# Order of work around eight points of a one-core kernel: attention and two gated products

## The chip, the core and the metric

The kernel runs on one core of a Trainium2 chip. The metric is device time in microseconds (us). A core has TensorE (PE in the profile; PEld is its weight load), VectorE (DVE), ScalarE (ACT), GpSimd (POOL) and SyncE (SP, which here only issues DMAs). Each engine works through its own list of instructions in order and waits on semaphores for the others. SBUF is the on-chip memory; a matmul writes into one of the eight banks of PSUM, from which ACT or DVE must copy the result out before the bank is used again.

## What is computed

All data is float32. Attention over chunks of 32 queries (4 batches, 8 heads, 768 positions, 64 wide), each chunk against 8 memory keys and a window of 56 keys, is followed by two gated layers over the 3072 tokens:

```python
scores = scale * np.matmul(q_c, k_full.transpose(0, 1, 3, 2))
a = np.exp(scores - max); a = a / (sum + 1e-9)
out[:, :, c_start:c_end] = np.matmul(a, v_full)
...
a = x @ w1;  b = x @ w2          # 512 -> 1024
x = (a * b @ w3) @ w_out         # 1024 -> 1024 -> 512
...
a = x @ w_a; b = x @ w_b         # 512 -> 1536
return a * b @ w_out2            # 1536 -> 512
```

## The kernel before, in words

**Precision.** A float32 operand is split into a high part (a copy rounded by ACT, `split_hi`, L103) and a low part (DVE or POOL subtracts the high part, `split_lo`, L106). A product is three passes of matmuls: high by high, high by low, low by high (`PASSES`, pairs of weight part and data part).

**Weights** arrive as raw 64-bit words. A block is loaded by SP (`w_load`, L374 for the 1 MB blocks of the first stage, L368 to L371 for the 512 KB blocks of `w1` and `w2`), scaled by two ACT instructions (`w_scale`, L389 and L390), joined by two DVE instructions (`w_bits`, L394 and L395), and, where parts are needed, split (L431 on ACT, L425 on DVE). `w_tick` moves each block one step; calls to it stand at fixed places in the program. `BUFS["raw2"]` gives the buffers for raw 1 MB blocks.

**Stage 1** multiplies `w3` by `w_out` once: two halves of eight steps `k`, four banks each (`wps`). The first half consumes eight 1 MB blocks of `w3a`, which the text calls r0 to r7, the second four blocks of `w3b`, r8 to r11, each for two steps. Half-steps are counted by `g`. After a half, ACT and DVE copy its four banks out (`w_evict`, L559 and L560).

**Attention** is cut into 16 units `u` of two groups and run in slots that are strewn between the products of the stages (`attn_slot`). In order, a unit loads keys (`kraw`, L122), queries (`q`, L129, one buffer) and values (`v`, L142 and L148), copies the keys (DVE, L158), makes scores (PE, `sc`), takes the maximum, subtracts, exponentiates and norms (L196, L199, L210, L218 to L221), transposes (PE, `pt`, L232), copies that out of its banks (ACT, `p`, L238), multiplies with the values (PE, `xp`) and splits the result into the layer's data `xt` (ACT L103, DVE L106).

**Stage 2** (tiles 0 to 3 of 512 tokens): eight `ab_step`s per tile, each two products `psA` and `psB` of twelve matmuls (`ab_half`), their gate, and then the second product `psY`. `between` is called after each half and runs a weight tick and attention slots.

**Stage 3** (tiles 4 and 5 as a pair) uses seven half-size products for the pair in place of eight (`seven12`, `product`, L892). It goes through the hidden dimension in two halves `h`. Each half ends with eight groups j of `psY`; the second half adds what the first one stored. Meanwhile `x_build` loads the next stage's data and splits it (L714 load, L722 subtraction, L103, L106).

**Stage 4** (three pairs of tiles): twelve blocks `f` per pair, each seven products p0 to p6 of six matmuls (`seven`) into banks `pa`, `pb`, `pc`, the gate (`times`, L1081 DVE, L1082 ACT, L1083 POOL), and `out_part` (`ops`). In a block, `copied` (ACT, L904) brings p0 out of its bank for p2 to start in it, and again p2 and p3; `plus` (DVE, L1076) does the other banks. `w7_hi` and `w7_lo` split the weights of the next block, and `other` advances a generator of side work.

The program is written out by hand in this order; no scheduler changes it. SP's list is in order too: a load that waits for its buffer holds all loads behind it.

Of the kernel before, what the change touches and what calls it, by code (L numbers as in the profile page):

```python
# [7 lines left out]
F32 = mybir.dt.float32  # L8
# [5 lines left out]
P = 128  # L14
# [9 lines left out]
TT = 512  # L24
# [14 lines left out]
CH = 512  # L39
BUFS = {"raw64": (3, 0), "raw2": (0, 4), "dec": (4, 3)}  # L40
SPLIT = 2
# [5 lines left out]
def tile_attention_moe(  # L47
# [32 lines left out]
    def dram_tile(n, shape):  # L80
        return dram.tile(shape, F32, name=n, tag=n)

    yd = [dram_tile(f"yd{i}", [P, KD, TT]) for i in range(NT1)]
    xd = {i: dram_tile(f"xd{i}", [P, KD, TT]) for i in range(ND, NT1)}

# [207 lines left out]
    for u in range(NA):  # L293
        t0, t1, t2, t3 = SLOTS.get(u, (8, 8, 11, 12))
        for s, stage_of in (
            (t0, a_trans),
            (t1, a_pt),
            (t3, a_x),
            (t2, a_pv),
            (t2, lambda u: a_v(u + 1)),  # L300
            (0, a_scores),
            (0, lambda u: a_q(u + 1)),
            (int(u > 0), a_max),
            (2, a_norm(0)),
            (2 + (u > 0), a_norm(1)),
            (int(u > 0), a_exp(0)),
            (int(u > 0), a_exp(1)),
        ):
            at(BASE[u] + s, (stage_of, u))
        if u > 0:  # L310
            at(BASE[u] - 3, (a_keys, u))
            at(BASE[u] - 2, (a_k, u + 1))
    at(0, (a_v, 0))
    NEED = []
# [4 lines left out]

    def attn_slot(n=1):  # L320
        for _ in range(n):
            s = acount[0]
            if s >= NEED[-1]:
                return
            acount[0] += 1
            for stage_of, u in todo.get(s, []):
                stage_of(u)

# [233 lines left out]
    for half in range(2):  # L562
        banks = [psd.tile([P, 512], F32, tag="d", name="wps") for _ in range(4)]
        for k in range(8):
            for m in range(4):
# [12 lines left out]
                if half == 0:  # L578
                    if g >= 9:
                        attn_slot()  # L580
                    if g in (0, 2, 4, 6, 8, 9):
                        w_tick()
                    if g == 0:
                        a_k(0)
                        a_q(0)
                    if g == 7:
                        a_keys(0)
                        a_k(1)
                    if g == 9:
                        bound[0] = len(wsrc)  # L590
                    if g == 13:
                        w_turn()
                else:
                    attn_slot()
                    if g == 0:
                        w_next()
                    if g in (1, 4, 5, 6, 9, 10, 11, 12):
                        w_tick()
# [12 lines left out]
    def ab_half(ps, w, j, rhs):  # L611
        i = 0
        for k in range(KD):
            for a, b in PASSES:
                mm(ps[:, :TT], w[:, a, j, (k + 2 * j) % KD, :], rhs[:, b, k, :], i == 0, i == 3 * KD - 1)
                i += 1

# [65 lines left out]
    def between():  # L683
        nstep[0] += 1
        b = nstep[0] - NB * ti
        n = nstep[0]
        converting = any(pipe) or wraw
        if converting:
            w_tick()
        attn_slot(min(NEED[-1], NEED[0] + -(-(NEED[-1] - NEED[0]) * n // NA1)) - acount[0])  # L690
        if not converting:
# [196 lines left out]
    def product(ps, i, w, first):  # L888
        n = 0
        for k in range(2):  # L890
            for a, b in PASSES:
                nc.tensor.matmul(  # L892
# [82 lines left out]
    for t in range(ND, NT1, 2):  # L975
        for h in range(2):
# [11 lines left out]
            groups = [(n, i) for n in range(KD) for i in range(2)]  # L988
            ps_of, olds = {}, {}

# [13 lines left out]

            def y_old(j):
                if h == 1 and j < len(groups):
                    olds[j] = y_load(tmp(), yd, t + groups[j][1], groups[j][0])

            y_old(0)
            y_old(1)  # L1010
            y_old(2)
            for j, (n, i) in enumerate(groups):
# [10 lines left out]
                ps = ps_of.pop(j)[:, :TT]  # L1023
                if h == 0:
                    z = copied(ps)
                else:
                    z = olds.pop(j)
                    onto(z, ps, z, ALU.add)
                nc.sync.dma_start(out=yd[t + i][:, n, :], in_=z)
                y_old(j + 3)  # L1030
                if h == 1:
# [47 lines left out]
    def times(x, y, g2):  # L1079
        z = tmp()  # L1080
        nc.vector.tensor_tensor(z, x, y, ALU.mult)  # L1081
        nc.scalar.activation(g2[:, 0, :], z, AF.Copy)  # L1082
        nc.gpsimd.tensor_tensor(g2[:, 1, :], z, g2[:, 0, :].bitcast(F32), ALU.subtract)  # L1083

    def seven(w, g1, g2, other, after, lead):

        pa, pb = bank(), bank()
        product(pa, 0, w, True)
        s1 = copied(pa)
        product(pb, 1, w, True)  # L1090
        c11 = plus(pb, s1)
# [13 lines left out]
        c12 = plus(pc, u2)  # L1105
        w7_lo()
        other(1)
        product(pa, 6, w, False)
        after()
        times(pa, c11, g1)  # L1110
        times(c12, c22, g2)

    def out_part(ops, f, g2):
# [26 lines left out]
    next(cw)  # L1140

    def other(n):
        for _ in range(n):
            next(cw, None)

    seq = list(range(0, NT1, 2))
    for si, t in enumerate(seq):
# [16 lines left out]
        while len(fo) < M2:  # L1164
            next(cw)
        ops2 = out_new(psd, "d")
        out_part(ops2, 0, g2[0])
# [9 lines left out]
        if si == 0:  # L1177
            stagestack.close()


# [81 lines left out]
```

## Time and profile before

| | before |
|---|---|
| runs | 1062.44 us median of 3 (1061.69 to 1063.23) |
| profiled execution | 1062.38 us, of which the span from first to last instruction 1060.6 |
| PE busy | 1045.2 us of the span, granted clock 1.000 throughout |
| DVE, ACT, POOL busy | 591.4, 449.1, 245.6 us |
| DMA | 153 MB; 364 GB/s in the first fortieth of the span, 144 on average |

A row of the timeline gives start and length of a run of equal instructions on one engine, in us from the span's start; in brackets stands how long the engine was idle before and what ended it. "x48" counts instructions. A float32 matmul of stage 1 and of attention leaves two records.

### The profile page before, as it was taken

The page shows a single profiled execution, that of the slowest core. Times are in us where ns is not written, and L with a number is a line of the kernel's source. Part 1 is how long each engine was busy: PE and PEld are TensorE (multiplying, and loading weights), DVE is VectorE, ACT ScalarE, POOL GpSimd, SP SyncE. Part 2 cuts the span into 40 slices and gives each one's busy share as a digit, 9 for nine tenths or more (in the row PEclk, how much of TensorE's full clock was granted, in tenths as well). Part 3 has the DMA queues.
Part 4 walks back from the last instruction along what each step waited for, and adds up shares of the span by engine and source line. Part 5 has one row for each costly group of instructions (what it writes and reads, how often), then busy time and mean ns, then how long its engine had stood idle before and what let it go on. Part 6 is the DMA issues. An engine that isn't in the chain of part 4 may idle for free.

```text
span 1060.6 us, 18308 instructions
## 1 busy us (share of the span) xinstructions
PE 1045.2 (99%) x7394; PEld 835.6 (79%) x7394; DVE 591.4 (56%) x950; ACT 449.1 (42%) x789; POOL 245.6 (23%) x264
## 2 busy tenths in 40 slices
PE   9999999999999999999899999999999999999998
PEld 3447788888888888888688888888888888888886
DVE  5868956676675346357755565544444454444410
ACT  6655622444443334344455545333333334343310
POOL 0102398222322000000032233013332202222210
PEclk9999999999999999999999999999999999999999
DMA  9974467768885423235733333322222223222211
GB/s 364 316 195 154 150 206 228 248 227 277 273 292 179 138 85 113 74 118 177 218 123 110 109 117 115 120 75 76 98 71 70 94 97 109 69 70 70 70 40 40
DMA packets 74997, 153.15 MB, mean 144 GB/s; under 512 B 7968, under 2 KB 38048, under 8 KB 73632
## 3 DMA queue, kind: packets, MB, share of 16 engines
q1 hardware_dynamic: 66640, 118.90, 34.1%
q0 software_dynamic: 8064, 33.03, 9.6%
q8 instruction: 58, 0.95, 0.4%
q14 instruction: 27, 0.22, 0.1%
q10 hardware_dynamic: 208, 0.04, 0.0%
HBM read 116.83 MB, written 35.13 MB: 143 GB/s over the span
## 4 chain that ended last, share of the span: by engine, by line
PE 90%; DMA 3%; DVE 3%; issue 1%; ACT 1%; SPq 0%; DVEq 0%; ACTq 0%
PE ps L892 39%; PE ops L94 18%; PE psY L94 11%; PE psB L94 7%; PE psA L94 7%; PE wps L94 3%; PE xp L94 2%; PE sc L94 1%; DMA q<-in_qt 1%; DMA raw<-in_w 1%; DMA raw<-in_w3a 1%; PE pt L232 1%; DVE w L425 1%; DVE dec L395 0%; DVE x L106 0%
## 5 line engine op out<-in xcount | busy, mean ns | idle before, releaser
L892 PE MATMUL ps<-x,w 128*128 128x512 f32 x1848 | 425.8, 389 | 3.3 <-DVE tmp L908 2.0
L892 PEld LDWEIGHTS ps<-x,w 128*128 128x128 f32 x1848 | 346.5, 188 | 76.7 <-ACT tmp L904 2.2
L1076 DVE TENSOR_TENSOR tmp<-ps,tmp 128x512 f32<-128x512 f32 x108 | 74.6, 691 | 142.9 <-PE ps L892 131.6
L106 DVE TENSOR_TENSOR w<-w 128x512 fp32r<-128x512 f32 (+1 forms) x176 | 105.8, 619 | 82.8 <-ACT w L103 82.7
L904 ACT ACTIVATE tmp<-ps 128x512 f32<-128x512 f32 x132 | 78.7, 597 | 165.2 <-PE ps L892 155.2
L94 PE MATMUL psY<-g,wo 128*128 128x512 f32 x576 | 134.6, 391 | 0.0
L783 POOL DMA_DIRECT2D w<-wc x36 | 20.1, 559 | 466.9 <-PE ps L892 328.8
L94 PEld LDWEIGHTS psY<-g,wo 128*128 128x128 f32 x576 | 107.3, 188 | 22.6 <-DVE tmp L908 0.3
L94 PE MATMUL ops<-wo,g 128*128 128x512 f32 x504 | 118.6, 389 | 0.0
L94 PEld LDWEIGHTS ops<-wo,g 128*128 128x128 f32 x504 | 94.6, 188 | 19.6
L94 PE MATMUL psA<-xt,w 128*128 128x512 f32 x384 | 94.8, 395 | 0.8 <-DVE xt L106 0.5
L1083 POOL TENSOR_TENSOR g<-tmp,g 128x512 fp32r<-128x512 f32 x66 | 84.1, 1291 | 46.9 <-ACT g L1082 46.9
L94 PE MATMUL psB<-xt,w 128*128 128x512 f32 x384 | 93.9, 393 | 0.0
L103 ACT ACTIVATE w<-w 128x512 fp32r<-128x512 f32 (+1 forms) x176 | 92.1, 572 | 1.4 <-DMA w<-wd 1.4
L1082 ACT ACTIVATE g<-tmp 128x512 fp32r<-128x512 f32 x66 | 40.7, 633 | 109.9 <-DVE tmp L1081 109.9
L94 PEld LDWEIGHTS psA<-xt,w 128*128 128x128 f32 x384 | 70.8, 188 | 16.8 <-ACT xt L103 1.1
L94 PEld LDWEIGHTS psB<-xt,w 128*128 128x128 f32 x384 | 71.2, 188 | 15.0
L94 PE MATMUL ops<-fo,g 128*128 128x512 f32 x288 | 68.2, 389 | 0.0
L389 ACT ACTIVATE raw<-raw 128x512 f32<-128x512 f32 (+1 forms) x66 | 48.9, 741 | 33.3 <-DMA raw<-in_wab 17.2
L94 PEld LDWEIGHTS ops<-fo,g 128*128 128x128 f32 x288 | 54.1, 188 | 11.2
L94 PE MATMUL wps<-w_f 128*128 128x512 f32 x128 | 57.5, 599 | 0.2 <-DVE w_f L395 0.2
L103 ACT ACTIVATE x<-xb 128x512 fp32r<-128x512 f32 x56 | 32.2, 624 | 41.4 <-DVE xb L722 26.5
(74 smaller groups left out, 952.2 us busy)
## 6 DMA issues: line engine op xcount, KB each, us to landing
w<-wc POOLq DMA_DIRECT2D x36, 640.0 KB, 4.2
raw<-in_wab SPq DMA_DIRECT2D x24, 512.0 KB
v<-in_vw SPq DMA_DIRECT2D x64, 168.0 KB
w<-wc POOLq DMA_DIRECT2D x36, 256.0 KB, 3.8
kraw<-in_kt SPq DMA_DIRECT2D x16, 512.0 KB
raw<-in_w3a SPq DMA_DIRECT2D x6, 1024.0 KB
q<-in_qt SPq DMA_DIRECT2D x16, 384.0 KB
wc<-cs SPq DMA_DIRECT2D x12, 512.0 KB
```

What stands on the lines that cost most here:

```text
L94: nc.tensor.matmul(o, lhsT=l, rhs=r, start=first, stop=last)
L103: nc.scalar.activation(hi, src, AF.Copy)
L106: nc.vector.tensor_tensor(lo, src, hi.bitcast(F32), ALU.subtract)
L232: nc.tensor.transpose(pt[:, a // 4, a % 4, :], t[:, a].rearrange("p r k -> p (r k)"), id_sb)
L389: nc.scalar.activation(h, h, AF.Prelu, scale=2.0**-112, alpha=2.0**32)
L425: nc.vector.tensor_tensor(lo, a, hi.bitcast(F32), ALU.subtract)
L783: (nc.gpsimd if c else nc.sync).dma_start(out=t[:, 1, :C7].bitcast(F32), in_=wseq[n][:, :C7])
L892: nc.tensor.matmul(ps, lhsT=w[i][:, a, k, :], rhs=xs[i][:, b, k, :], start=first and n == 0, stop=n == 5, skip_group_check=not first,)
L904: nc.scalar.activation(z, ps, AF.Copy)
L1076: nc.vector.tensor_tensor(z, ps, y, ALU.add)
L1082: nc.scalar.activation(g2[:, 0, :], z, AF.Copy)
L1083: nc.gpsimd.tensor_tensor(g2[:, 1, :], z, g2[:, 0, :].bitcast(F32), ALU.subtract)
```

## The change

Eight edits in one file; line numbers after the first shift by one or more (L389 becomes L403 and so on).

1. `raw2`: three buffers for raw 1 MB blocks, not four.
2. In stage 1 three weight steps move: the one at `g == 13` of the first half to 14, those at 11 and 12 of the second to 13 and 14.
3. In `between`, the slots' products, bank copies and loads come ahead of the weight tick, the soft-max's steps and key loads behind it (`attn_slot(n, True)`, `attn_rest`).
4. `ab_half` and `product` go through a whole pass before the next; the first tile's first step takes low weights before low data.
5. The second half of the pair no longer loads and adds the first half's `y`: both are copied out by ACT and stored apart (`yh`, `yd`).
6. A generator `y_sums` adds the two in stage 4, beside the second pair.
7. `times` only multiplies; the split of the gate is done by `g_rest` after the next block's first `copied`.
8. The last `w7_lo` and `other` of a block come after `times`.

```diff
-BUFS = {"raw64": (3, 0), "raw2": (0, 4), "dec": (4, 3)}
+BUFS = {"raw64": (3, 0), "raw2": (0, 3), "dec": (4, 3)}
...
-    def attn_slot(n=1):
+    held_back = []
+
+    def attn_slot(n=1, later=False):
...
-            for stage_of, u in todo.get(s, []):
-                stage_of(u)
+            for stage_of, u, soft_part in todo.get(s, []):
+                if later and soft_part:
+                    held_back.append((stage_of, u))
+                else:
+                    stage_of(u)
+
+    def attn_rest():
+        for stage_of, u in held_back:
+            stage_of(u)
+        held_back.clear()
...
-                    if g == 13:
+                    if g == 14:
                         w_turn()
...
-                    if g in (1, 4, 5, 6, 9, 10, 11, 12):
+                    if g in (1, 4, 5, 6, 9, 10, 13, 14):
                         w_tick()
...
     def ab_half(ps, w, j, rhs):
-        i = 0
-        for k in range(KD):
-            for a, b in PASSES:
-                mm(ps[:, :TT], w[:, a, j, (k + 2 * j) % KD, :], rhs[:, b, k, :], i == 0, i == 3 * KD - 1)
-                i += 1
+        order = ((0, 0), (1, 0), (0, 1)) if nstep[0] == 0 else PASSES
+        for i, (a, b) in enumerate(order):
+            for k in range(KD):
...
         converting = any(pipe) or wraw
+        goal = min(NEED[-1], NEED[0] + -(-(NEED[-1] - NEED[0]) * n // NA1))
+        attn_slot(goal - acount[0], True)
         if converting:
             w_tick()
-        attn_slot(min(NEED[-1], NEED[0] + -(-(NEED[-1] - NEED[0]) * n // NA1)) - acount[0])
+        attn_rest()
...
     def product(ps, i, w, first):
         n = 0
-        for k in range(2):
-            for a, b in PASSES:
+        for a, b in PASSES:
+            for k in range(2):
...
-                if h == 0:
-                    z = copied(ps)
-                else:
-                    z = olds.pop(j)
-                    onto(z, ps, z, ALU.add)
-                nc.sync.dma_start(out=yd[t + i][:, n, :], in_=z)
-                y_old(j + 3)
+                z = copied(ps)
+                nc.sync.dma_start(out=(yd if h else yh)[t + i][:, n, :], in_=z)
...
     def times(x, y, g2):
         z = tmp()
         nc.vector.tensor_tensor(z, x, y, ALU.mult)
-        nc.scalar.activation(g2[:, 0, :], z, AF.Copy)
-        nc.gpsimd.tensor_tensor(g2[:, 1, :], z, g2[:, 0, :].bitcast(F32), ALU.subtract)
+        gated.append((z, g2))
+
+    def g_rest():
+        for z, g in gated:
+            split_hi(g[:, 0, :], z)
+            nc.gpsimd.tensor_tensor(g[:, 1, :], z, g[:, 0, :].bitcast(F32), ALU.subtract)
+        gated.clear()
...
         product(pa, 0, w, True)
         s1 = copied(pa)
+        g_rest()
         product(pb, 1, w, True)
...
         c12 = plus(pc, u2)
-        w7_lo()
-        other(1)
         product(pa, 6, w, False)
         after()
         times(pa, c11, g1)
         times(c12, c22, g2)
+        w7_lo()
+        other(1)
...
+    def y_sums():
+        for n in range(KD):
+            for i in range(ND, NT1):
+                x, y = y_load(tmp(), yd, i, n), y_load(tmp(), yh, i, n)
+                yield
+                yield
+                nc.vector.tensor_tensor(x, x, y, ALU.add)
+                nc.sync.dma_start(out=yd[i][:, n, :], in_=x)
+                yield
+                yield
+                yield
...
         if si == 0:
             stagestack.close()
+            cw = y_sums()
```

The first place is SP's list in stage 1, from the third block on; `raw` are the 1 MB blocks (the first two rows of each list are r3 and r4). Before:

```order
L374 DMA raw_135<-in_w3a 128x2048
L374 DMA raw_146<-in_w3a 128x2048
L374 DMA raw_154<-in_w3a 128x2048
L374 DMA raw_167<-in_w3a 128x2048
L122 DMA kraw<-in_kt 128x2x512
L129 DMA q<-in_qt 128x2x384
L374 DMA raw_181<-in_w3a 128x2048
L374 DMA raw_192<-in_w3b 128x2048
L374 DMA raw_202<-in_w3b 128x2048
L122 DMA kraw<-in_kt 128x2x512
L374 DMA raw_217<-in_w3b 128x2048
L129 DMA q<-in_qt 128x2x384
```

The same list of the changed kernel, from r3 on:

```order
L388 DMA raw_146<-in_w3a 128x2048
L388 DMA raw_154<-in_w3a 128x2048
L388 DMA raw_167<-in_w3a 128x2048
L123 DMA kraw<-in_kt 128x2x512
L130 DMA q<-in_qt 128x2x384
L388 DMA raw_181<-in_w3a 128x2048
L388 DMA raw_192<-in_w3a 128x2048
L388 DMA raw_202<-in_w3b 128x2048
L123 DMA kraw<-in_kt 128x2x512
L388 DMA raw_217<-in_w3b 128x2048
L130 DMA q<-in_qt 128x2x384
```

Each load of keys and queries now stands behind one block fewer: the first `q` behind r5 and not r6, the second behind r9 and not r10.

The second place is ACT's list at the end of stage 1; `p` is unit 2's copy out of the transposes' banks, `wo` the copies of the second half's banks, `xt` the data of stage 2's first tile. Before:

```order
L431 ACTIVATE w_681<-dec 128x512
L389 ACTIVATE raw_662<-raw_662 128x512
L390 ACTIVATE raw_662<-raw_662 128x512
L431 ACTIVATE w_681<-dec 128x512
L389 ACTIVATE raw_675<-raw_675 128x512
L390 ACTIVATE raw_675<-raw_675 128x512
L238 ACTIVATE p_713<-pt 128x768
L559 ACTIVATE wo<-wps 128x512 x3
L103 ACTIVATE xt<-xp 128x4x128
L103 ACTIVATE xt<-xp 128x4x64
```

And in the changed kernel:

```order
L239 ACTIVATE p_695<-pt 128x768
L445 ACTIVATE w_699<-dec 128x512
L403 ACTIVATE raw_664<-raw_664 128x512
L404 ACTIVATE raw_664<-raw_664 128x512
L573 ACTIVATE wo<-wps 128x512
L445 ACTIVATE w_699<-dec 128x512
L403 ACTIVATE raw_677<-raw_677 128x512
L404 ACTIVATE raw_677<-raw_677 128x512
L573 ACTIVATE wo<-wps 128x512 x2
L104 ACTIVATE xt<-xp 128x4x128
L104 ACTIVATE xt<-xp 128x4x64
```

The copy `p` has moved ahead of two weight ticks, and these now stand between the bank copies.

The third place is ACT's list where stage 3 passes into stage 4, from the pair's fifth copied group on (`x` and `xb` are the next stage's data, `ps` the banks of block 0 and 1). Before, ACT had no `psY` there:

```order
L103 ACTIVATE x_5295<-xb 128x512
L103 ACTIVATE x_5296<-xb 128x512
L103 ACTIVATE x_5294<-xb 128x512
L103 ACTIVATE x_5297<-xb 128x512
L904 ACTIVATE tmp<-ps_5526 128x512 x2
```

In the changed kernel (x_5297 is there what was x_5295):

```order
L104 ACTIVATE x_5297<-xb 128x512
L925 ACTIVATE tmp<-psY 128x512
L104 ACTIVATE x_5298<-xb 128x512
L104 ACTIVATE x_5296<-xb 128x512
L104 ACTIVATE x_5299<-xb 128x512
L925 ACTIVATE tmp<-psY 128x512 x3
L925 ACTIVATE tmp<-ps_5520 128x512 x2
```

ACT has taken over from DVE the eight copies of `psY`, four of which stand here; the last three come right ahead of block 0's first copy.

## Rows read from the trace of the kernel before

**Rows 1.** The page, busy time and share of the span.

```profile
PE 1045.2 (99%) x7394; PEld 835.6 (79%) x7394; DVE 591.4 (56%) x950; ACT 449.1 (42%) x789; POOL 245.6 (23%) x264
```

**Rows 2.** Timeline of PE: the rows with idle time, and one without.

```profile
40.20 1.18 PE L94 MATMUL sc<-kw,q 64*32 64x64 f32 x96 [1.58 <-DMA q<-in_qt]
...
75.43 1.60 PE L94 MATMUL xp<-p,v 64*64 64x32 f32 x96 [1.94 <-ACT p L238]
...
79.27 0.51 PE L94 MATMUL psA<-xt,w 128*128 128x512 f32 x1 [0.32 <-ACT xt L103]
80.27 2.79 PE L94 MATMUL psA<-xt,w 128*128 128x512 f32 x11 [0.50 <-DVE xt L106]
...
108.19 2.88 PE L94 MATMUL psB<-xt,w 128*128 128x512 f32 x12
112.94 1.60 PE L94 MATMUL xp<-p,v 64*64 64x32 f32 x96 [1.86 <-ACT p L238]
...
124.68 0.85 PE L232 MATMUL pt<-id_sb,t 96*128 96x96 f32 x8 [0.41 <-DVE xt L106]
...
515.17 1.61 PE L892 MATMUL ps<-x,w 128*128 128x512 f32 x6 [1.29 <-DVE tmp L908]
517.49 11.18 PE L892 MATMUL ps<-x,w 128*128 128x512 f32 x48 [0.70 <-DVE tmp L908]
530.00 7.10 PE L892 MATMUL ps<-x,w 128*128 128x512 f32 x30 [1.34 <-ACT tmp L904]
```

**Rows 3.** The chain that ended last, one piece of stage 4: start, length.

```profile
539.82 9.52 PE ps L892 x42
```

**Rows 4.** Timeline of ACT in stage 1: it starts on r2, on r4.

```profile
12.29 1.13 ACT L389 ACTIVATE raw<-raw 128x1024 f32<-128x1024 f32 x1 [1.19 <-DMA raw<-in_w3a]
...
17.34 1.18 ACT L389 ACTIVATE raw<-raw 128x1024 f32<-128x1024 f32 x1 [0.34 <-DMA raw<-in_w3a]
```

**Rows 5.** Timeline of DVE in stage 1: r2, unit 0's mask, r8.

```profile
14.50 1.23 DVE L395 CUSTOM_DVE_ANT_0 w_f<-raw,w_f 128x2048 uint16<-128x2048 uint16 x1 [0.34 <-ACT raw L390]
...
27.50 0.29 DVE L182 TENSOR_TENSOR sc<-sc,mask_sb 32x128 f32<-32x128 f32 x1 [0.65 <-PE sc L94]
...
37.44 1.22 DVE L395 CUSTOM_DVE_ANT_0 w_f<-raw,w_f 128x2048 uint16<-128x2048 uint16 x1
```

**Rows 6.** Timeline of all engines, end of stage 3: loads of 256 KB, and their user.

```profile
502.89 2.77 SPq L714 DMA_DIRECT2D xb<-yd  x4
...
506.40 0.63 ACT L103 ACTIVATE x<-xb 128x512 fp32r<-128x512 f32 x1 [1.05 <-DMA xb<-yd]
```

**Rows 7.** Timeline of ACT around two copies p.

```profile
71.81 0.68 ACT L389 ACTIVATE raw<-raw 128x512 f32<-128x512 f32 x1 [3.56 <-DMA raw<-in_w]
...
74.58 0.81 ACT L238 ACTIVATE p<-pt 128x768 f32<-128x768 f32 x1
...
109.43 1.14 ACT L210 ACTIVATE t<-t 96x512 f32<-96x512 f32 x2
...
112.10 0.79 ACT L238 ACTIVATE p<-pt 128x768 f32<-128x768 f32 x1
```

**Rows 8.** Busy time by stretch: core, us, then busy us (x instructions) of each engine.

```profile
core 0: us, PE busy (x) PEld busy (x) DVE busy (x) ACT busy (x) POOL busy (x), PEclk, DMA share, GB/s
...
84.00:125.00 41.00, 38.73 (x465) 31.38 (x455) 38.41 (x60) 26.88 (x48) 12.38 (x9) 1.00 0.56 178
```

**Rows 9.** Timeline of ACT, end of stage 3 and block 1 of stage 4.

```profile
513.25 2.19 ACT L103 ACTIVATE x<-xb 128x512 fp32r<-128x512 f32 x4 [0.57 <-DVE xb L722]
...
528.29 1.17 ACT L1082 ACTIVATE g<-tmp 128x512 fp32r<-128x512 f32 x2 [2.35 <-DVE tmp L1081]
```

**Rows 10.** Timeline of DVE in block 1 of stage 4.

```profile
530.59 1.48 DVE L106 TENSOR_TENSOR fo<-dec,fo 128x512 fp32r<-128x512 f32 x1
...
534.47 0.69 DVE L1076 TENSOR_TENSOR tmp<-ps,tmp 128x512 f32<-128x512 f32 x1 [0.27 <-ACT w L103]
```

**Rows 11.** Timeline of POOL in block 1 of stage 4.

```profile
529.01 2.51 POOL L1083 TENSOR_TENSOR g<-tmp,g 128x512 fp32r<-128x512 f32 x2 [2.12 <-ACT g L1082]
```

More of the change, by code (lines that the diff above doesn't have):

```diff
@@ L83, in tile_attention_moe @@
     yd = [dram_tile(f"yd{i}", [P, KD, TT]) for i in range(NT1)]
+    yh = {i: dram_tile(f"yh{i}", [P, KD, TT]) for i in range(ND, NT1)}
     xd = {i: dram_tile(f"xd{i}", [P, KD, TT]) for i in range(ND, NT1)}
@@ L302, in tile_attention_moe @@
             (0, lambda u: a_q(u + 1)),
+        ):
+            at(BASE[u] + s, (stage_of, u, False))
+        for s, stage_of in (
             (int(u > 0), a_max),
@@ L308, in tile_attention_moe @@
         ):
-            at(BASE[u] + s, (stage_of, u))
+            at(BASE[u] + s, (stage_of, u, True))
         if u > 0:
-            at(BASE[u] - 3, (a_keys, u))
-            at(BASE[u] - 2, (a_k, u + 1))
-    at(0, (a_v, 0))
+            at(BASE[u] - 3, (a_keys, u, True))
+            at(BASE[u] - 2, (a_k, u + 1, True))
+    at(0, (a_v, 0, False))
     NEED = []
@@ L611, in ab_half @@
     def ab_half(ps, w, j, rhs):
-        i = 0
-        for k in range(KD):
-            for a, b in PASSES:
-                mm(ps[:, :TT], w[:, a, j, (k + 2 * j) % KD, :], rhs[:, b, k, :], i == 0, i == 3 * KD - 1)
-                i += 1
+        order = ((0, 0), (1, 0), (0, 1)) if nstep[0] == 0 else PASSES
+        for i, (a, b) in enumerate(order):
+            for k in range(KD):
+                mm(
+                    ps[:, :TT],
+                    w[:, a, j, (k + 2 * j) % KD, :],
+                    rhs[:, b, k, :],
+                    i == 0 and k == 0,
+                    i == 2 and k == KD - 1,
+                )
     def ab_step(w, rhs, g2, between):
@@ L988, in tile_attention_moe @@
             groups = [(n, i) for n in range(KD) for i in range(2)]
-            ps_of, olds = {}, {}
+            ps_of = {}
             def y_some(j, m0, m1):
@@ L1003, in y_some @@
                         )
[L1005 to L1011, printed above, removed]
             for j, (n, i) in enumerate(groups):
@@ L1081, in times @@
         nc.vector.tensor_tensor(z, x, y, ALU.mult)
-        nc.scalar.activation(g2[:, 0, :], z, AF.Copy)
-        nc.gpsimd.tensor_tensor(g2[:, 1, :], z, g2[:, 0, :].bitcast(F32), ALU.subtract)
+        gated.append((z, g2))
+    gated = []
+    def g_rest():
[3 more added lines that the diff above has]
+        gated.clear()
     def seven(w, g1, g2, other, after, lead):
@@ L1165, in tile_attention_moe @@
             next(cw)
+        g_rest()
         ops2 = out_new(psd, "d")
```

## The prediction

> **What bounds the kernel now.** The first look is at the busy line: PE works 99% of the span, DVE 56%, ACT 42% [rows 1]. PE's number of matmuls is the same in both programs, and the granted clock is 1.000 already, so only time in which PE stands still can be won. The second look is at the chain: a piece of 42 matmuls in 9.52 us, 0.2267 us each, with nothing between them [rows 3]. The third is PE's timeline, where the reader should look at the brackets alone: nine waits in the whole program, 9.94 us together [rows 2]. A printed wait is a little short, since the end of the last matmul before it is drawn late: the twelve from 108.19 are drawn as 2.88 us, at the pace they take 2.72 [rows 2, 3]. So a wait costs 0.16 us more than its bracket, and all that can be won is 9.94 + 9 x 0.16, about 11.4 us. Each wait then has its own question: what is late there, what does the edit bring forward, and what is late next.
>
> **A. The load of q (1.74 us).** PE waits at 40.20 for `q` [rows 2]. In the new order `q` stands behind r9, not r10, so it lands in time. The price is the third buffer: with four, r5 waited for no later block than r1, and with three it can be issued only when r2 has been converted, 14.50 + 1.23 = 15.73 [rows 5]. The pace of loading: ACT starts on r2 at 12.29 and on r4 at 17.34, each time on a landing, so a 1 MB block takes 2.52 us [rows 4]. What a load takes beyond the pace: four of 256 KB issued from 502.89 have their first user start at 506.40, after 3.51 us, of which 0.63 is pace; 2.88 is fixed [rows 6]. These loads come from the same queue, in another stage. Then r5 lands at 15.73 + 2.88 + 2.52 = 21.13; `kraw`, `q` and r6 (0.5, 0.375 and 1 MB) take 4.73 more, so r6 lands at 25.86. From landing to converted r2 took 15.73 - 12.29 = 3.44 [rows 4, 5]; r6 is converted at 29.30. DVE's list is in order, and unit 0's mask stands behind that: it started at 27.50, and now starts at about 29.35. From mask to r8 converted DVE took 37.44 + 1.22 - 27.50 = 11.16 [rows 5], and the first half's bank copy now stands ahead of r8 too (0.6). So r8 is ready at 41.1. The scores at 40.20 end at 41.38, where the second half begins [rows 2]; without any wait that would be at 39.64. The wait moves from `q` to r8's conversion, and the gain is **0.3**. If the fixed time is nil, the whole 1.74 is won; if r6 or r7 comes another 0.8 late, 0.5 is lost.
>
> The rows give a load 2.88 us beyond its pace. The Trainium skill (DMA: Bandwidth & Descriptors, "Anatomy of one DMA — SWDGE (gpsimd) path") states about 2.0 us fixed and bytes over 436 GB/s, for loads that GpSimd issues; these are SP's. By it r6 would land 1.2 us earlier and A would be worth an estimated 1.5, which is nearly the first rival. I keep the rows' figure.
>
> **B and C. The end of stage 1 (2.10 and 1.14 us).** At 75.43 PE waits for ACT's `p`, which starts at 74.58; ahead of it stand two weight ticks, the first of which waited 3.56 us idle for its block and began at 71.81 [rows 2, 7]. The copy `p` now stands ahead of that idle time and needs nothing but the transposes, done by then: all 2.10 us go. PE then comes to the first `psA` at 79.27 - 0.32 - 2.10 = 76.85. Ahead of the data's high part ACT now has eight instructions from 71.81 on; two in a row take 1.14 [rows 7], so they end near 76.4 and the data near 77.0: 0.2 is left of the first wait. The second, for the low part on DVE, has gone: the pass with low data is last, and eight matmuls, 1.81 us, lie ahead of it. B and C together **3.0**, between 2.0 (C's waits come back through later ACT work) and 3.24.
>
> **D and E. Two waits in stage 2 (2.02 and 0.57 us).** At 112.94 PE waits for `p`, which ACT starts at 112.10 after a weight tick; the two `t` ahead end at 109.43 + 1.14 = 110.57 [rows 2, 7]. With the tick behind, `p` is 1.53 earlier. At 124.68 the wait is for DVE. From 84 to 125 DVE is busy 38.41 of 41 us [rows 8]: it is the second bound here, and when PE comes 1.5 earlier, DVE must too. The low part of `xt` moves ahead of a tick's two DVE instructions, about what PE gains. I take 1.5 for D and 0.1 for E: **1.6**, from 0 (DVE gives back all of it) to 2.6.
>
> **F. From stage 3 to 4 (1.45 and 0.86 us).** At 515.17 and 517.49 PE waits for DVE, which drains the last `psY` banks by adds [rows 2]. Now ACT copies them (0.6 each, like its `x` copies [rows 6]), eight copies for eight adds, and eight loads of 256 KB go. But ACT has its own work there: four `x` from 513.25 to 515.44, which waited for DVE's low parts [rows 9]. Those come 0.6 to 1.2 earlier, with DVE freed. Then the copy of the fifth group is done by 513.8; the sixth group's comes after three `x`, at 515.4 to 516.0; then two more copies and block 0's first. PE would need its bank at 515.17 - 1.45 = 513.72 and 1.4 later. Of 2.31 us between 0.5 and 1.2 stay; I take 0.9 and win **1.4**; ends 0.5 (ACT's `x` no earlier) and 2.31.
>
> **G. Block 1 of stage 4 (1.50 us).** At 530.00 PE waits for the copy of p0, behind which ACT's order was at fault: it stood 2.35 us idle for DVE's second product of the gate, until 528.29, made the gate's two high parts, and only then the copy [rows 2, 9]. Now the copy comes first, and DVE's products come ahead of `w7_lo`. The wait goes: **1.5**, at least 1.0 if block 0 hands something on.
>
> **What is added.** `y_sums` makes eight adds (0.69 each, like L1076 [rows 10]), sixteen loads and eight stores, in the second pair, where the weights are no longer converted, so DVE has the time. Loads are two steps ahead of their add; they take about 3.5 us [rows 6], a block some 9.5 for its seven products [rows 3]. Cost nothing; without this cover an add stands at the head of DVE's list for its load, `plus` queues behind it and PE behind that, at most a few us in all. The gate's parts come one block later than their maker and have a product's time before `out_part`: nothing. SP's queue is shorter in stage 3.
>
> The sum: 0.3 + 3.0 + 1.6 + 1.4 + 1.5 = 7.8 us. The profiled execution took 1062.38, so **1054.6**; its 0.06 to the median doesn't matter.
>
> **Rivals.** *R1, loads land sooner:* if r6 is no later than DVE's own work, A gives 1.7, and if the `x` of F come early, F 2.3: 2.3 us more, **1052.3**. For it: 2.88 us comes from another stage's loads. Against: the third buffer binds six blocks in a row.
>
> *R2, DVE holds stage 2:* DVE is busy 94% there [rows 8]. If its conversions don't start earlier when PE does, the 3.0 us of B and C come back as waits at `psA`, `psB`, `xp` or `pt`, and **1057.6** is left. For it: that share. Against: only one wait there names DVE today.
>
> *R3, slower: POOL meets DVE.* The gate's low parts, two POOL subtractions, now run beside DVE's two-input work in every block. In block 1 this can be seen: POOL is at it from 529.01 to 531.52, and DVE's `fo`, 0.69 long like its neighbours, takes 1.48 and ends 0.55 behind POOL [rows 10, 11]. DVE stood still for POOL. The Trainium skill (SBUF — State Buffer, "SBUF: two separate sides") has it as a rule: a GpSimd instruction and a DVE instruction with two SBUF inputs take a shared port pair exclusively, for the whole instruction; the trace agrees. Is there room? From a block's start: p0 ends at 1.36, its copy at 1.96, the first high part at 2.55, POOL at 5.2; `fo` 0.55 later, two `w` low parts and `plus` (0.69 each) end at 7.8. They are due when p6 starts: 1.36 x 6 = 8.16. Today's block shows the same closeness, `plus` ending at 535.16 for a p6 due at 530.00 + 4 x 1.36 = 535.44 [rows 2, 10]. So 0.3 is left. A further POOL operation in the way (2.51 / 2 = 1.26 [rows 11]) would cost 0.9 in each of eleven blocks of the first pair, 10 us: **1064.7**. The gain is eaten up from 0.7 us a block beyond the margin.
>
> **Chances.** The sum as it stands 0.5; R1 0.2; R2 0.2; R3 0.1, half of it the whole price, half enough to leave no change. The likeliest case alone: 1053.0 to 1056.2 (A, F and E by half their bounds). The range runs from R1 to R2, each with 0.8 for the spread of the runs around their median: 1051.5 to 1058.4; outside stay R3 and the far ends of the first two. What a measurement of this kernel can tell from no change is some 0.2%, 2.1 us. All cases but R3 are below that: faster 0.91, same 0.05, slower 0.04.
>
> **What would show it.** A: the scores without a wait, but the second half's first matmuls waiting for DVE near 41. B, D: `p` right behind the transposes, `xp` at about 73.3, then 108 or so. C: no DVE wait at the first `psA`. F: `psY` copies on ACT, 0.5 to 1.2 us of waits near 514. G: the copy of p0 with no wait in block 1, and POOL beside DVE in each block. I would be wrong if PE waits for r6 or r7 inside the first half, if new waits stand between 77 and 125, or if p6 waits in the blocks of stage 4.

## The result, and the profile after

The changed kernel takes 1054.25 us (median of 6 runs, 1052.55 to 1056.74) against 1063.13 before in the same measurement: a ratio of 0.9919, 95% interval 0.9904 to 0.9934. The forecast was 1054.6. The profiled execution's span is 1052.3 us, 8.3 less than the 1060.6 before; the sum had said 7.8.

The busy line first, against [rows 1]:

```profile
PE 1045.2 (99%) x7394; PEld 835.9 (79%) x7394; DVE 595.1 (57%) x950; ACT 446.5 (42%) x797; POOL 250.4 (24%) x264
```

PE's work is the same to a tenth; only its idle time has shrunk. The timeline of PE, the rows with idle time and two without (compare the nine of [rows 2]):

```profile
23.08 3.70 PE L95 MATMUL wps<-w_f 128*128 128x512 f32 x8 [0.24 <-DVE w_f L409]
...
35.42 3.70 PE L95 MATMUL wps<-w_f 128*128 128x512 f32 x8 [0.46 <-DVE w_f L409]
...
40.25 1.18 PE L95 MATMUL sc<-kw,q 64*32 64x64 f32 x96 [0.18 <-DMA q<-in_qt]
41.37 4.13 PE L95 MATMUL wps<-w_f 128*128 128x512 f32 x9
...
73.48 1.60 PE L95 MATMUL xp<-p,v 64*64 64x32 f32 x96
...
77.31 3.02 PE L95 MATMUL psA<-xt,w 128*128 128x512 f32 x12 [0.32 <-ACT xt L104]
...
120.06 0.85 PE L233 MATMUL pt<-id_sb,t 96*128 96x96 f32 x8 [0.32 <-DVE xt L107]
...
510.71 18.05 PE L913 MATMUL ps<-x,w 128*128 128x512 f32 x78 [0.22 <-ACT tmp L925]
```

Both waits for `p` (B, D) are below what a row prints; the second wait at `psA`, the second at block 0 and the one in block 1 have gone. In stage 1 two waits stand that were not there: for the conversions of r4 and r7. DVE in stage 1, the second instruction of r6, unit 0's mask and the second instruction of r8; SP, the loads of r9 and of unit 1's `q`; and then DVE in blocks 0 and 1 of stage 4 and POOL in block 1 (compare [rows 10, 11]):

```profile
29.28 1.23 DVE L409 CUSTOM_DVE_ANT_0 w_f<-raw,w_f 128x2048 uint16<-128x2048 uint16 x1 [0.37 <-ACT raw L404]
30.54 0.29 DVE L183 TENSOR_TENSOR sc<-sc,mask_sb 32x128 f32<-32x128 f32 x1
...
40.05 1.23 DVE L409 CUSTOM_DVE_ANT_0 w_f<-raw,w_f 128x2048 uint16<-128x2048 uint16 x1
```

```profile
30.53 0.33 SPq L388 DMA_DIRECT2D raw<-in_w3b  x1
30.95 1.37 SPq L130 DMA_DIRECT2D q<-in_qt  x1
```

```profile
515.04 1.29 DVE L107 TENSOR_TENSOR w<-w 128x512 fp32r<-128x512 f32 x2 [1.88 <-ACT w L104]
...
522.95 0.78 DVE L107 TENSOR_TENSOR fo<-dec,fo 128x512 fp32r<-128x512 f32 x1 [0.20 <-ACT fo L104]
524.57 1.47 DVE L107 TENSOR_TENSOR w<-w 128x512 fp32r<-128x512 f32 x2 [0.84 <-ACT w L104]
526.14 0.69 DVE L1085 TENSOR_TENSOR tmp<-ps,tmp 128x512 f32<-128x512 f32 x1
```

```profile
521.89 3.00 POOL L1098 TENSOR_TENSOR g<-tmp,g 128x512 fp32r<-128x512 f32 x2 [1.70 <-ACT g L104]
```

r8 is ready at 41.28, where the second half begins. `q` is issued at 30.95, where it was 27.50 before: r9 ahead of it waits for a raw buffer, and is issued at 30.53, when r6 has been converted (30.51). So the scores start no earlier. In stage 4 POOL now works beside DVE, and both are a little longer for it: POOL's two subtractions take 3.00 us for 2.51, two `w` low parts 1.47 for 1.29.

Where the time came from, by marks on PE's timeline that both programs have (first matmul of the second half; first `psB`; the `psB` after the `pt` near 120; the long run of `psY` that ends stage 3, at 493.86 before; the first `ops`; the last run of `ops`), in us between them:

| stretch | before | after | won | forecast |
|---|---|---|---|---|
| start to second half (A) | 41.32 | 41.37 | -0.05 | 0.3 |
| to first `psB` (B, C) | 42.88 | 40.01 | 2.87 | 3.0 |
| to `psB` near 120 (D, E) | 41.12 | 39.31 | 1.81 | 1.6 |
| to the last `psY` of stage 3 | 368.54 | 368.56 | -0.02 | 0 |
| to the first `ops` (F, G) | 43.07 | 39.35 | 3.72 | 2.9 |
| to the last `ops` (stage 4) | 481.68 | 481.72 | -0.04 | 0 |

The first row holds 0.48 us that are not A's: the first matmul of `wps` started at 8.46 before and at 8.94 after, behind the same warm-up. Counted from there the first half took 32.86 and 32.43 us, 0.43 less.

### The profile page after: what moved, and what is told of

The parts are those of the page before. It is cut to its first block, busy times and chain, and to the rows that moved or that the text cites. A ratio compares the mean times of both kernels' runs of the same rounds, so it can differ in the third digit from the quotient of the medians.

```text
span 1052.3 us, 18316 instructions
## 1 busy us (share of the span) xinstructions
PE 1045.2 (99%) x7394; PEld 835.9 (79%) x7394; DVE 595.1 (57%) x950; ACT 446.5 (42%) x797; POOL 250.4 (24%) x264
## 4 chain that ended last, share of the span: by engine, by line
PE 91%; DMA 4%; DVE 2%; ACT 1%; issue 1%; SPq 0%; DVEq 0%; ACTq 0%
PE ps L913 40%; PE ops L95 19%; PE psY L95 11%; PE psB L95 7%; PE psA L95 7%; PE wps L95 3%; PE xp L95 2%; DMA raw<-in_w3a 2%; PE sc L95 1%; DMA raw<-in_w 1%; PE pt L233 1%; DMA q<-in_qt 1%; DVE dec L409 0%; DMA xb<-yd 0%; ACT raw L403 0%
## 5 line engine op out<-in xcount | busy, mean ns | idle before, releaser
L107 DVE TENSOR_TENSOR w<-w 128x512 fp32r<-128x512 f32 (+1 forms) x176 | 108.0, 631 | 79.7 <-ACT w L104 79.5
L1098 POOL TENSOR_TENSOR g<-tmp,g 128x512 fp32r<-128x512 f32 x66 | 88.8, 1360 | 150.3 <-ACT g L104 150.3
L403 ACT ACTIVATE raw<-raw 128x512 f32<-128x512 f32 (+1 forms) x66 | 49.0, 743 | 33.2 <-DMA raw<-in_wab 17.9
L104 ACT ACTIVATE g<-tmp 128x512 fp32r<-128x512 f32 x82 | 47.2, 624 | 19.1 <-DVE tmp L929 11.1
L404 ACT ACTIVATE raw<-raw 128x512 uint32<-128x512 uint32 (+1 forms) x66 | 49.0, 742 | 0.0
```

Of the source, the lines that this page charges most:

```text
L104: nc.scalar.activation(hi, src, AF.Copy)
L107: nc.vector.tensor_tensor(lo, src, hi.bitcast(F32), ALU.subtract)
L403: nc.scalar.activation(h, h, AF.Prelu, scale=2.0**-112, alpha=2.0**32)
L404: nc.scalar.activation(l, l, AF.Copy, scale=2.0**-29)
L1098: nc.gpsimd.tensor_tensor(g[:, 1, :], z, g[:, 0, :].bitcast(F32), ALU.subtract)
```

## The experiments

Times are medians; ratios are to the kernel before in the same measurement. Since one edit is worth 0.1 to 0.3%, the reading goes by the profile and the ratio only backs it.

**A: four buffers again.**

```diff
-BUFS = {"raw64": (3, 0), "raw2": (0, 3), "dec": (4, 3)}
+BUFS = {"raw64": (3, 0), "raw2": (0, 4), "dec": (4, 3)}
```

> The changed kernel with four raw buffers in place of three, its other edits kept. With the fourth buffer q stands behind r10 again. Theory (the second half of stage 1 starts when the later of q and r8's conversion is there, and the change only swapped one for the other): the waits for r4 and r7 inside the first half (0.41 and 0.62 us over the pace) go, the wait for q comes back with about 1.7, and the second half's first matmul stays within 0.3 us of 41.3 us, less what the warm-up's start differs; the whole time stays within 0.6 us of the changed kernel. Rival (the third buffer is what A won): the second half starts 0.4 us or more later than in the changed kernel and the time rises by as much.

1054.11 us, ratio 0.9907 (0.9894 to 0.9919). The waits for r4 and r7 go and `q` is late again, by 2.28 us; but something was not foreseen. PE's timeline, and busy time by stretch (columns as in [rows 8]):

```profile
40.76 1.54 PE L95 MATMUL sc<-kw,q 64*32 64x64 f32 x96 [2.28 <-DMA q<-in_qt]
42.23 6.67 PE L95 MATMUL wps<-w_f 128*128 128x512 f32 x12
```

```profile
40.00:42.00 2.00, 1.24 (x96) 1.27 (x96) 0.81 (x2) 0.00 (x0) 0.00 (x0) 0.85 0.22 35
42.00:45.00 3.00, 3.00 (x19) 1.35 (x7) 2.53 (x4) 0.69 (x2) 0.00 (x0) 0.53 0.98 351
```

Behind the wait the granted clock is 0.53, near the lower of TensorE's two levels (1.2 of 2.4 GHz), from 42 to 45 us. Twelve records of `wps` (six matmuls) take 6.67 us, where they take 5.42 at full clock (next experiment). So the second half starts at 42.23, 0.9 later than the theory's 41.3, and goes on slowly: a wait can cost more than its length. The whole time is still that of the changed kernel, as forecast; of the four executions the one profiled is the longest (1055.50 us, with a mean granted clock of 0.998, the others 0.999 or 1.000). In the profile of before, with a wait of 1.58 at this place, the clock stayed at 1.00:

```profile
42.00:45.00 3.00, 3.00 (x9) 1.33 (x8) 2.80 (x6) 1.60 (x3) 0.00 (x0) 1.00 0.91 330
```

**A: four buffers, and r10 and the rest behind q.**

```diff
-BUFS = {"raw64": (3, 0), "raw2": (0, 3), "dec": (4, 3)}
+BUFS = {"raw64": (3, 0), "raw2": (0, 4), "dec": (4, 3)}
...
-    bound = [NW0]
+    bound = [10]
...
+                    if g == 9:
+                        bound[0] = len(wsrc)
                     if g in (0, 2, 4, 6, 8, 9):
                         w_tick()
...
-                    if g == 9:
-                        bound[0] = len(wsrc)
```

> The changed kernel with four raw buffers, and with r10 held back until unit 1's q and unit 0's v have been issued. Theory (q is late because it stands in the queue behind a block that is needed only ten us later; r8 is late because of the third buffer): neither holds here, the second half starts at 39.6 to 40.2 us in place of 41.37, and 1.2 to 1.7 us are won against the changed kernel. Rival one (r8's conversion is late on DVE whatever the buffers are): it starts at 41.3 again. Rival two (r10 and r11 now come late): the wait moves to 47 to 52 us, with 0.5 us or more, and the whole time doesn't move.

1054.02 us, 0.9904 (0.9890 to 0.9917). PE's timeline:

```profile
38.70 1.19 PE L95 MATMUL sc<-kw,q 64*32 64x64 f32 x96
39.83 5.42 PE L95 MATMUL wps<-w_f 128*128 128x512 f32 x12
...
56.79 1.59 PE L95 MATMUL sc<-kw,q 64*32 64x64 f32 x96 [2.26 <-DMA q<-in_qt]
58.31 6.62 PE L95 MATMUL wps<-w_f 128*128 128x512 f32 x12
```

The second half starts at 39.83 with no wait: with four buffers, `q`'s place in the queue decides. That the fourth buffer is needed too is argued, from r8, which three buffers let be ready only at 41.28; no run has the new place with three. But the freed bound also let r11 and stage 2's first weights ahead of unit 2's keys and queries, and `q` is late there, with the slow clock behind it again (x12 in 6.62, not 5.42). The second rival held in kind, for another load.

**B to E: the weight tick first in each gap of stage 2.**

```diff
+        if converting:
+            w_tick()
-        attn_slot(goal - acount[0], True)
-        if converting:
-            w_tick()
-        attn_rest()
+        attn_slot(goal - acount[0])
```

> The changed kernel with the weight tick ahead of all attention work again in each gap of stage 2, and nothing else undone. Stage 1 keeps its order. Theory: D comes back (1.5 to 1.8 us at the xp near 108), B does not (its two ticks stand in stage 1 and moved by the steps of g), and the time rises by 1.5 to 2.0 us. Rival (what is won at one gap is eaten at the next, since DVE is busy 94% there): the sum of waits between 77 and 125 us grows by less than 0.7.

1057.18 us, 0.9930 (0.9918 to 0.9942).

```profile
110.87 1.60 PE L95 MATMUL xp<-p,v 64*64 64x32 f32 x96 [1.69 <-ACT p L239]
...
123.28 0.85 PE L233 MATMUL pt<-id_sb,t 96*128 96x96 f32 x8 [1.08 <-DVE xt L107]
```

D is back and B is not. From `psB` to `psB` the stretch takes 41.60 us for 39.31, 2.3 more, where 1.5 to 2.0 were expected: 1.6 at D and 0.8 at E, which is worse than in the kernel before (a wait of 1.08 for 0.41). What was won was not eaten at the next gap.

**F: DVE adds the halves in stage 3.**

```diff
...
-                z = copied(ps)
-                nc.sync.dma_start(out=(yd if h else yh)[t + i][:, n, :], in_=z)
+                if h == 0:
+                    z = copied(ps)
+                else:
+                    z = olds.pop(j)
+                    onto(z, ps, z, ALU.add)
+                nc.sync.dma_start(out=yd[t + i][:, n, :], in_=z)
+                y_old(j + 3)
...
-            cw = y_sums()
+            cw = iter(())
```

> The changed kernel with the pair's second half added by DVE as before, its loads with it, and no sums in stage 4. Theory (F): the two waits at the start of stage 4 come back, 2.3 us over the pace in place of 0.38, and the time rises by 1.9. Rival (the sums in stage 4 cost something that the waits don't show): it rises by 1.0 or less.

1058.34 us, 0.9943 (0.9930 to 0.9956).

```profile
512.56 1.61 PE L913 MATMUL ps<-x,w 128*128 128x512 f32 x6 [1.29 <-DVE tmp L929]
514.87 5.51 PE L913 MATMUL ps<-x,w 128*128 128x512 f32 x23 [0.70 <-DVE tmp L929]
```

Both waits return to the hundredth of a microsecond as in [rows 2]. From the last `psY` run to the first `ops` it takes 41.83 us for 39.35, 2.5 more, where 1.9 was expected: part of the excess is that the matmul behind a waiting one starts late too (at 515.21, 0.34 us after the one at 514.87, where the pace is 0.23). From the first `ops` to the last `ops` nothing is won by leaving the sums out (481.59 us; with them 481.57 to 481.72 in the profiles whose stage 4 is the changed kernel's): `y_sums` costs nothing that can be seen.

**G: the gate split at once, `w7_lo` ahead of the last product.**

```diff
-        gated.append((z, g2))
+        split_hi(g2[:, 0, :], z)
+        nc.gpsimd.tensor_tensor(g2[:, 1, :], z, g2[:, 0, :].bitcast(F32), ALU.subtract)
...
+        w7_lo()
+        other(1)
         product(pa, 6, w, False)
         after()
         times(pa, c11, g1)
         times(c12, c22, g2)
-        w7_lo()
-        other(1)
```

> The changed kernel with the gate split at once in the block that makes it, and with the weights' low parts ahead of the last product, as before. Theory (G, one wait in block 1): the wait for the copy of p0 in block 1 comes back with 1.0 to 1.5 us and no other; the time rises by that. Rival (all blocks gain a little from the later split, as their ends are less crowded): waits in several blocks, 2 us or more. Rival two (DVE is freed by the other edits, so block 1's wait does not return): no change, within 0.3.

1056.11 us, 0.9923 (0.9908 to 0.9937), which can't be told from the changed kernel. The one wait that returns:

```profile
521.82 2.35 PE L913 MATMUL ps<-x,w 128*128 128x512 f32 x9 [0.44 <-ACT tmp L925]
```

It is 0.44 us, not 1.34. Neither rival held as put; the theory's place is right and its size is not. Over the pace it is 0.60 us of G's 1.50: the other 0.9 stay away without edits 7 and 8. With F undone and these two kept (above) no wait stands in block 1 either, so either set covers the 0.9 by itself.

**Pass order.**

```diff
-        order = ((0, 0), (1, 0), (0, 1)) if nstep[0] == 0 else PASSES
-        for i, (a, b) in enumerate(order):
-            for k in range(KD):
+        for k in range(KD):
+            for i, (a, b) in enumerate(PASSES):
...
-        for a, b in PASSES:
-            for k in range(2):
+        for k in range(2):
+            for a, b in PASSES:
```

> The changed kernel with passes as the inner loop again in both places, all else kept. Theory (pass order only covered the second wait at the first psA): 0.5 to 0.8 us come back there, nothing in stages 3 and 4; the time rises by 0.5 to 1.0. Rival (in stage 4 a product's first matmuls now need low parts four matmuls earlier, and w7_lo has moved behind the gate): waits of 0.2 us or more in many of the blocks, 3 us or more in all.

1055.70 us, 0.9924 (0.9910 to 0.9939).

```profile
79.81 2.36 PE L95 MATMUL psA<-xt,w 128*128 128x512 f32 x9 [0.50 <-DVE xt L107]
...
513.99 2.19 PE L912 MATMUL ps<-x,w 128*128 128x512 f32 x8 [0.39 <-ACT tmp L924]
```

From the second half to the first `psB` it takes 40.83 us for 40.01: 0.8, as expected. From the last `psY` run to the first `ops` it takes 39.95 us for 39.35, another 0.6 at block 0 (the wait shown, and a shorter one at 511.95 that no row prints), which was not expected; in the blocks after it nothing comes back.

**R3: POOL's subtractions twice.** The second subtraction repeats the first.

```diff
             nc.gpsimd.tensor_tensor(g[:, 1, :], z, g[:, 0, :].bitcast(F32), ALU.subtract)
+            nc.gpsimd.tensor_tensor(g[:, 1, :], z, g[:, 0, :].bitcast(F32), ALU.subtract)
```

> The changed kernel with each of the two POOL subtractions of a block made twice, so POOL works some 6 us in place of 3 beside DVE's weights. Theory (the profile of the changed kernel: POOL's operations get longer, 1.5 in place of 1.26 us, and DVE's two-input ones by 0.1 each, so plus ends 0.5 us ahead of p6): DVE is later by 0.4 us at most, PE doesn't wait, the time stays within 1 us. Rival (R3 of the prediction: DVE stands still for whole POOL instructions, 0.3 us is left): p6 waits 0.9 us or more in eleven blocks of the first pair at least, 10 us or more.

1086.10 us, 1.0210 (1.0193 to 1.0227): some 32 us more than the changed kernel. My expectation fell, and the prediction's rival was right in kind. DVE, POOL and PE, in block 1 and in the last pair:

```profile
524.00 2.58 DVE L107 TENSOR_TENSOR w<-w 128x512 fp32r<-128x512 f32 x2 [0.84 <-ACT w L104]
526.50 0.68 DVE L1085 TENSOR_TENSOR tmp<-ps,tmp 128x512 f32<-128x512 f32 x1
...
995.92 3.52 DVE L107 TENSOR_TENSOR w<-w 128x512 fp32r<-128x512 f32 x2 [1.81 <-ACT w L104]
```

```profile
526.11 1.61 POOL L1099 TENSOR_TENSOR g<-tmp,g 128x512 fp32r<-128x512 f32 x1
```

```profile
527.24 1.66 PE L913 MATMUL ps<-x,w 128*128 128x512 f32 x6 [0.41 <-DVE tmp L1085]
...
986.19 1.66 PE L913 MATMUL ps<-x,w 128*128 128x512 f32 x6 [1.34 <-DVE tmp L1085]
```

The same two low parts take 1.29 us alone, 1.47 in the changed kernel, 2.58 and 3.52 here, and `plus` behind them comes late for p6 in 32 of the 36 blocks. `plus` itself, with one of its inputs in PSUM, keeps its 0.68 us beside POOL. The span grows by 31.4 us. A block of 12.24 us takes 12.97 in the first pair, 12.70 in most of the second and 13.90 in most of the third. The prediction had worked out 0.9 for one further POOL operation in the way, in the eleven blocks of the first pair alone; two are added here, cost 0.7 there, and the dearest blocks are in the pairs that it left out. Why the pairs differ stays open.

**Both orders mended.** Four buffers; r10 alone behind `q`, then unit 2's keys and queries, then r11; and the data's high part ahead of the third bank copy.

```diff
-BUFS = {"raw64": (3, 0), "raw2": (0, 3), "dec": (4, 3)}
+BUFS = {"raw64": (3, 0), "raw2": (0, 4), "dec": (4, 3)}
...
-    bound = [NW0]
+    bound = [10]
...
-                if k == 7 and m > 0:
+                if k == 7 and m > 0 and (half, m) != (1, 3):
                     w_evict(half, m - 1)
...
+                    if g == 9:
+                        bound[0] = 11
                     if g in (0, 2, 4, 6, 8, 9):
                         w_tick()
...
                     attn_slot()
+                    if g == 15:
+                        w_evict(half, 2)
```

> The changed kernel with four raw buffers, r10 alone let through behind unit 1's q and unit 0's v, then unit 2's keys and queries, then r11 and the weights of stage 2; and at the end of stage 1 the data's high part ahead of the third bank copy on ACT. Theory (q's place in the queue was what cost e2_q_before_r10 its second wait): the second half starts near 39.8 us, no wait of over 0.5 us near 56, no wait at the first psA (0.48 today); 1.5 to 2.0 us better than the changed kernel where its second half starts at 41.37. Rival (the queue is full: whatever comes first, something lands late): a wait of 1 us or more moves to r10, r11 or unit 2's q, and less than 0.7 is won.

1051.98 us, 0.9885 (0.9869 to 0.9901). A second measurement:

> The kernel of e9_both once more. If its stage 1 (31.18 us from the first to the 65th matmul of wps) is owed to q's place in the queue, it is within 0.3 us of that again and the time 1.0 to 1.3% below the kernel before; if it was a lucky execution, it is 32.4 or more, and the time is that of the changed kernel, 0.8% below.

1051.64 us, 0.9880 (0.9863 to 0.9896). From the first to the 65th record of `wps` (where the second half begins): 31.18 and 30.90 us.

```profile
38.46 1.20 PE L95 MATMUL sc<-kw,q 64*32 64x64 f32 x96
39.59 5.42 PE L95 MATMUL wps<-w_f 128*128 128x512 f32 x12
...
54.23 1.19 PE L95 MATMUL sc<-kw,q 64*32 64x64 f32 x96
```

No wait at either `q`, and none at the first `psA`. It is the best of the versions: both intervals lie below the changed kernel's 0.9904 to 0.9934. That is of another measurement, in which before was faster (1063.13 us for 1063.91 and 1064.52); by the times alone, eight executions take 1051.11 to 1052.86 us, the changed kernel's six 1052.55 to 1056.74. The 0.56 us won at `psA` came back in the first profile as a wait of 0.56 for DVE's keys at 113.84, and in the second hardly (0.17 over the pace): from `psB` to `psB` these two take 39.89 and 39.13 us, the changed kernel 39.31.

**The kernel before, twice more.** No edit.

> The kernel before, profiled once more, to see how far stage 1 differs from one execution to the next: from the first to the 65th matmul of wps it took 32.86 us in the profile shown, and 32.43 to 34.05 in six profiles with three raw buffers (the changed kernel and those experiments that leave its stage 1 alone). Theory (A won nothing that stands out from this spread): 32.4 to 34 here too. Rival (A's order costs time in stage 1): 32.9 or less again.

> The kernel before a third time, for the same question: theory 32.4 to 34 us from the first to the 65th matmul of wps, rival 32.9 or less.

1066.31 and 1064.24 us. From the first to the 65th record of `wps` it took 32.32 and 32.05 us, with 32.86 in the profile shown, as the rival said. The first of the two has more to tell. PE's timeline, and busy time by stretch:

```profile
75.71 2.79 PE L94 MATMUL xp<-p,v 64*64 64x32 f32 x96 [2.53 <-ACT p L238]
78.43 3.78 PE L94 MATMUL wps<-w_f 128*128 128x512 f32 x4
...
115.62 2.14 PE L94 MATMUL xp<-p,v 64*64 64x32 f32 x96 [2.09 <-ACT p L238]
117.69 4.02 PE L94 MATMUL psA<-xt,w 128*128 128x512 f32 x12
```

```profile
76.00:79.00 3.00, 3.00 (x97) 2.87 (x93) 1.29 (x2) 0.62 (x2) 0.00 (x0) 0.50 0.47 155
79.00:82.00 3.00, 3.00 (x5) 0.96 (x3) 0.76 (x2) 1.36 (x3) 0.00 (x0) 0.50 0.71 179
...
116.00:120.00 4.00, 4.00 (x90) 3.50 (x84) 3.83 (x5) 2.22 (x5) 3.16 (x3) 0.57 0.51 149
```

Here B's and D's waits are followed by a granted clock of 0.50 and 0.57. From the start of the first `xp` to the first `psA` it takes 5.97 us, in the profile of [rows 2] 3.84. In the second execution the waits at the same two places are 1.48 and 2.05 us, and the clock falls behind both:

```profile
75.00:79.00 4.00, 4.00 (x99) 2.50 (x100) 1.29 (x2) 1.35 (x4) 0.00 (x0) 0.70 0.59 178
...
112.00:116.00 4.00, 2.49 (x97) 2.43 (x98) 3.73 (x9) 4.00 (x8) 2.55 (x2) 0.77 0.49 148
116.00:120.00 4.00, 4.00 (x15) 3.23 (x16) 4.00 (x5) 2.13 (x5) 1.38 (x2) 0.81 0.74 185
```

## Why the prediction was right, step by step

**A** is the term whose working the runs do not bear out. One part of its working came out: r8 was ready at 41.28 (41.1 forecast), 0.1 us before PE came to it. That was luck in part. r6's first user started at 27.01 and r6 was converted at 30.51, not 25.86 and 29.30: the sum took 2.88 us beyond the pace from loads of another stage, and here the loads of r4 and r5 were still on their way. The error was made good by DVE, which needed 10.7 us from the mask to r8, not 11.8. `q` did not land in time: PE still waits 0.18 us for it. That it would was put down without a working, and the third buffer, which holds r9 back until r6 is converted, has `q` issued 3.45 us later than before. The buffer also delays r4, which the prediction passed over: ACT starts on it at 19.58, where it was 17.34. And "PE waits for r6 or r7", named as a sign of error, came true for r4 and r7.

Over executions: the six profiles whose stage 1 is the changed kernel's took 32.43, 33.92, 33.93, 32.66, 34.05 and 32.73 us from the first to the 65th record of `wps`, mean 33.3; the three of before 32.4. So in the pair of profiles shown A won 0.43 us, while on average the first half seems to be 0.9 longer. With ranges that overlap (32.05 to 32.86 before) and profiles of several measurements this is likely, not shown; nor is it shown which of edits 1 and 2 it would be, as four buffers with edit 2 took 33.54. Two of the three long ones have late first scores (0.70 and 1.52 us, for unit 0's keys), the third a wait of 0.91 for `q`; why the loads land so unevenly is open. R1 did not happen in stage 1: the loads landed later than worked out, not sooner.

**B, C, D, E** came out as forecast, 4.68 us for 4.6. B has no experiment of its own: its `xp` starts at 73.48 (73.3 forecast), and no profile with edit 2 prints a wait there, while the three of before wait 1.94, 2.53 and 1.48 us. C kept 0.48 over the pace where 0.2 was forecast; D kept 0.26. R2 did not happen. Busy time by stretch in the changed kernel, columns as in [rows 8]:

```profile
84.00:125.00 41.00, 40.59 (x457) 32.97 (x456) 39.02 (x61) 27.24 (x48) 14.01 (x10) 1.00 0.54 169
```

DVE is busy 39.02 us there, more than the 38.41 before, and its work still moved ahead with PE. Only 0.6 us in one profile of the mended version shows what R2 feared.

**F and G** won 3.72 for 2.9. The term that was mis-sized is F: 0.38 remains, below the 0.5 to 1.2 that I had set for it. ACT's `x` copies came 1.14 us earlier (18.25 us behind the start of the last `psY` run, 19.39 before), near the far end of my 0.6 to 1.2. That is 1.9 for F and 1.5 for G. Most of the other 0.3 is what the 0.16 for a wait leaves out: behind each wait the second step is slow as well (0.34 us at 530.34 before, where the pace is 0.23). G's wait went whole; the experiment shows that 0.6 of it needs G's own edits and 0.9 goes by F's as well, so the two terms are not independent.

**What is added** cost nothing: 481.72 us for 481.68 over stage 4.

**R3** had the right mechanism, and the margin decided against it: `plus` ends at 526.83 and p6 starts at 528.60 - 1.36 = 527.24, so 0.41 was left, 0.3 forecast. That DVE's two-input operations stand still for POOL is shown by doubling it. The Trainium skill (SBUF — State Buffer, "SBUF: two separate sides") says the loser waits for the whole instruction; two low parts at 3.52 us, 2.23 more than alone, agree with that, while in the changed kernel the same pair lost only 0.18, as most of POOL's time lay where DVE had nothing with two SBUF inputs to do.

**The list of waits** was one short: PE also waits 0.18 us at 15.78 for `w_f` in the kernel before. It changes nothing in the sum.

**What the sum could not hold:** it was made against one profiled execution, whose clock never fell. In two other executions of before B's and D's waits are followed by a slower clock, while the six profiles with the changed kernel's stage 1 keep a granted clock of 1.00 from 20 to 130 us. The executions of before that were measured beside the experiments say how often: of 29, eight have a mean granted clock of 1.000 and take 1061.62 to 1063.91 us (mean 1062.7), 21 have 0.995 to 0.998 and take 1062.94 to 1066.41 (mean 1064.7). The changed kernel's six have 0.999 or 1.000. So the median gain of 8.9 us most likely holds some clock that was won back, which no term of the sum has, and probably less of A. That 8.9 and 7.8 agree so well is in part luck: F and G won 0.8 more than forecast, the clock added to it, and A gave less.

## What to carry to other kernels

Follow each wait to what ends last, then ask what is late next on that engine; in the two profiles every group came out so within 0.9 us. When a load is late, look at its place in the queue before its buffers: here, with two blocks moved behind it, the first half of stage 1 is 1.4 us shorter than before, where the order with one buffer less won nothing that stands out. Take what a wait costs from several executions: the clock can fall behind it in one and not in the next. Where an operation moves beside another engine that can hold it up, work out the margin before the next user, and double the intruder to see the price: here a margin of 0.4 us a block stood between no cost and 31 us.

## What was not expected of the hardware

The clock falls behind some waits of PE and not behind others. Waits of 1.94 and 1.86 us in the profile of before, and of 1.69 in the run with the tick first, left it at 1.00. Waits of 2.26, 2.28 and 2.09 in other executions were followed by 0.53 to 0.57 in stretches of 3 to 4 us, one of 2.53 by 0.50 over the six from 76 to 82 us, one of 2.05 by 0.77 and 0.81 in the stretches from 112 to 120, and one of 1.48 by 0.70 from 75 to 79. What decides is open; the length of the wait alone does not. At the start of the program the five warm-up matmuls (ten records), the same in both kernels, ended at 8.40 us before and 9.10 after, and at 8.84 and 9.38 in the two further executions of before. Between the two profiles that moves the first real matmul by 0.48 us without any edit.
